# Attention by pairs of heads on two-bank PSUM tiles, Mish on two chunks at once, and a new order of steps

## The chip, the cores and the metric

The kernel runs on one core of a Trainium2 chip. A core has five engines with an instruction queue each: TensorE (PE; PEld is its weight load), VectorE (DVE), ScalarE (ACT), GpSimd (POOL) and SyncE (SP), which here issues the DMAs. The metric is the time of one execution on the device in microseconds (us), as the median of several runs.

## What is computed

Eight batches of eight heads, 576 tokens, 64 features a head. Heads 0 to 3 look back over the last 32 tokens, heads 4 to 7 over every fourth of the last 128. The result, 4608 tokens by 512 features, goes through a feed-forward network with the Mish activation.

```python
scores = scale * np.matmul(q, k.transpose(0, 1, 3, 2))
rel = pos[:, None] - pos[None, :]
mask_plain = (rel >= 0) & (rel < window)                        # 32, heads 0-3
mask_dil = (rel >= 0) & (rel < window * dilation) & (rel % dilation == 0)   # 4, heads 4-7
scores = np.where(masks[None, :, :, :], scores, -1000000000.0)
attn = softmax(scores)                                          # + 1e-9 in the denominator
x = (attn @ v).transpose(0, 2, 1, 3).reshape(B * S, H * D)      # 4608 x 512
h = x @ w_in                                                    # 512 -> 2048
g = h * np.tanh(log1p(exp(h)))                                  # Mish
out = g @ w_out                                                 # 2048 -> 512
```

## The kernel before

**Precision.** Inputs and output are fp32. Operands are split into an fp16 high and low part, and a product is three fp16 matmuls (low·high, high·low, high·high), with power-of-two scales (`f`, `s`) from the largest absolute value of each operand.

**Tiling.** The work is cut into 16 units u = 0 to 15, each half a batch (288 tokens, all heads). A unit goes through these steps, each a Python generator that issues its instructions up to the next `yield` when it is called:

- `ld`, `lv`: DMA loads of q, k, v (on SP's queue). `pr`: largest values (`amax`, DVE), their maximum over partitions, the scales, and the fp16 parts of q, k and v. From unit 6 on the maximum over partitions (tile mru) is POOL's `partition_all_reduce`.
- `sp` and `sc`: the matmuls of the scores of a pair of heads (tiles psc), then mask and maximum on DVE. `ex`: exp on ACT. `tp`: fp16 parts of the weights and a DMA transpose. `va`: the product with v (tile pav), the denominator (den on ACT), and its reciprocal and the normalised output (rec, xs on DVE). `tx`: fp16 parts of xs and a DMA transpose into x, the unit's FFN input. `sp` and `tx` go by pairs of heads; `sc`, `ex`, `tp` and `va` by single heads 0 to 7.
- `ff u.fc`: FF1 of one chunk of 128 of the 2048 features: 12 matmuls of 128x128x288, and Mish on ACT into hm. `gt u.j`: the gated value of four chunks in two fp16 parts (ACT and DVE). `fs`: per-unit scales of FF1 and FF2 (fs, sg, fo).
- `fo u.e.j`: FF2, 12 matmuls for output chunk e (of 4) and feature group j (of 4). After j = 3 the sum is evicted into y (ACT, a few on DVE), and `out_T<-y` stores it. y has two buffers.

In units 0 to 3 ("direct") the attention is in fp32 and is transposed on TensorE. Beside these units, 16 parts of the weights are loaded and split (`wl`, `wm`, `ww`, `ws`, `wp`); `ws` gives the scales f_1 and f_o. `kw n` issues n matmuls of zeros that compute nothing and keep TensorE busy.

**Order.** Nothing is reordered by a scheduler: under `tc.manual_schedule` the list ORDER, some 2,700 words written out in the file, is gone through word by word, and each word runs its step to the next yield. Each engine works through its own queue in that order and waits by semaphores.

**PSUM.** Eight banks of 512 fp32 columns: four one-bank tiles in rotation for the attention (tag "a"), and four one-bank tiles f0 to f3 in rotation for FF1 and FF2.

```python
    fbs, f_turn = [ps.tile([P, 512], F32, name=f"f{i}", bufs=1) for i in range(4)], [-1]
```

In the lists of instructions further on, tiles are named by what the program calls them (b0_70 is tile b0), a DMA or instruction by its line.

Of the kernel before, what the change touches and what calls it, by code (L numbers as in the profile page):

```python
# [42 lines left out]
ws0.0 va0.7 va0.7 tx0.0 ws0.0 tp0.4 tx0.0 tp0.5 tp0.4 kw4 tx0.0 ww0.0.0 kw1 tx0.3 tx0.0 tp0.5 kw7 sp0.1 tx0.3 wm0.2.0
kw1 tx0.3 ld1 sc0.2 va0.4 sc0.3 va0.4 kw6 ex0.2 tx0.3 pr1 ex0.3 ex0.2 va0.5 wp0.0.1 tp0.2 va0.4 tp0.2 fs0.0 ex0.3
wp0.0.1 kw16 kw16 kw2 va0.2 wm0.1.0 tp0.3 ww0.2.0 wl0.2.1 va0.2 va0.5 tp0.3 va0.5 va0.2 kw16 kw16 va0.3 ww0.1.0 tx0.2
va0.3 tx0.2 va0.3 fs0.3 kw16 kw1 tx0.1 tx0.2 ww0.1.0 tx0.1 tx0.2 kw11 tx0.1 kw1 sp1.0 tx0.1 wp0.0.0 ff0.12 sc1.0 sc1.1
ex1.0 sp1.1 wp0.0.0 pr1 tp1.0 ff0.13 sc1.3 tp1.0 wl0.1.1 ex1.1 ld2 wm0.2.1 pr1 sc1.2 kw2 pr1 ff0.0 lv2 ex1.3 ww0.2.1
ex1.2 pr1 ff0.12 ff0.15 ww0.2.0 tp1.1 va1.0 tp1.1 ws0.2 ff0.13 va1.0 ff0.15 sp1.3 va1.0 ff0.0 ws0.2 wm0.1.1 ff0.14
sc1.7 wp0.2.0 sc1.6 sp1.2 ff0.14 ww0.2.1 ex1.7 kw2 va1.1 ff0.3 ff0.1 sc1.4 wp0.2.1 ff0.2 sc1.5 ex1.6 va1.1 gt0.3
ww0.1.1 tp1.2 va1.1 kw5 ws0.1 wp0.2.0 ex1.4 ex1.5 tx1.0 tp1.4 tp1.2 wp0.2.1 wl1.3.0 ff0.3 kw6 va1.2 ws0.1 kw9 ff0.8  # L50
tx1.0 ww0.1.1 tp1.4 tx1.0 ff0.2 tp1.5 ff0.9 tx1.0 wp0.1.0 gt0.3 va1.4 ff0.1 kw2 tp1.3 tp1.5 kw1 ff0.11 va1.2 wp0.1.0
va1.4 wp0.1.1 va1.2 wl1.3.1 tp1.3 wp0.1.1 wm1.3.0 kw16 va1.3 wl1.1.0 va1.5 fs0.2 va1.5 kw3 ff0.4 wl1.1.1 va1.3 va1.4
gt0.0 va1.3 va1.5 tp1.6 ff0.8 tp1.7 fs0.1 tx1.1 ff0.9 ff0.7 pr2 tp1.6 tp1.7 tx1.1 va1.6 ff0.11 va1.7 ff0.4 tx1.2
ww1.3.0 lv3 ff0.10 va1.6 va1.7 va1.6 wm1.3.1 fs1 ff0.6 tx1.1 ff0.7 va1.7 tx1.2 ww1.3.1 tx1.3 ff0.10 tx1.2 gt0.0 ff0.5
tx1.3 tx1.2 ww1.3.0 tx1.3 sp2.0 tx1.3 gt0.2 pr2 ff1.8 sc2.0 ff0.5 ws1.3 sc2.1 ff1.8 ff0.6 gt0.2 gt0.1 ff1.10 pr2
wm1.1.0 ws1.3 pr2 ff1.0 ex2.0 pr2 ff1.9 gt0.1 ex2.1 ff1.1 ww1.3.1 ff1.0 tp2.0 tp2.1 sp2.1 ff1.10 pr3 ff1.9 ff1.4
wm1.1.1 ld3 tp2.0 sc2.2 ff1.7 wp1.3.0 ww1.1.0 sc2.3 ff1.11 ff1.1 wp1.3.0 ff1.4 ff1.2 tp2.1 ff1.7 ww1.1.0 wl1.2.0
ff1.11 sp2.3 wp1.3.1 ff1.3 ff1.2 ww1.1.1 ex2.2 wp1.3.1 ff1.5 sc2.6 fo0.3.0 wl1.2.1 ww1.1.1 gt1.2 fo0.3.1 ex2.6 ws1.1
sc2.7 ex2.3 wm1.2.0 va2.0 ws1.1 sp3.2 va2.0 fo0.3.2 sc3.4 fs2 tp2.2 wm1.2.1 ww1.2.0 fo0.3.3 va2.0 ex3.4 ww1.2.1 va2.1
gt1.2 ff1.6 ff1.3 sc3.5 ws1.2 ff1.5 ww1.2.0 fo0.3.3 gt1.0 fo0.3.3 ff1.12 va2.1 wp1.1.0 ff1.14 ws1.2 ff1.12 ff1.13  # L60
va2.1 tp2.2 wp1.1.0 va2.2 sp3.1 va2.2 gt1.0 ff1.6 wl1.0.1 wp1.1.1 tp2.3 ff1.15 sc3.2 wp1.2.0 wp1.1.1 fo0.1.0 gt1.1
va2.2 wl1.0.0 fo0.1.1 sc3.3 tp2.3 gt1.1 ff1.15 tp2.6 va2.3 tp2.6 sp3.0 va2.3 ff1.14 va2.3 tx2.0 sc3.1 fo1.3.0 tx2.0
ff1.13 sc3.0 ex3.3 va2.6 fo1.3.1 tx2.0 wp1.2.0 va2.6 ex2.7 sp2.2 ww1.2.1 wm1.0.0 tp2.7 fo0.1.2 wm1.0.1 fo0.1.3 tp2.7
ww1.0.1 gt1.3 ww1.0.0 fo1.1.0 fo0.1.3 sc2.5 fo0.1.3 fo1.3.2 sc2.4 ld4 va2.6 ex2.4 fo0.2.0 gt1.3 ex2.5 ww1.0.1 ws1.0
# [154 lines left out]
def attn_mish_ffn_kernel(  # L219
# [692 lines left out]
    def ff2(u, e, j):  # L912

        d = U[u]
        if j == 0:
            d["po", e] = f_next()
# [88 lines left out]
```

## Time and profile before

| what | value |
|---|---|
| median of 3 runs | 925.51 us (925.34 to 926.61) |
| span of the profiled execution | 923.6 us, 22682 instructions; its own time is not listed |
| granted TensorE clock | 0.999 |
| busy: PE, PEld | 913.6 us (99%), 738.9 us |
| busy: DVE, ACT, POOL | 648.8 us (70%), 563.4 us (61%), 17.5 us (2%) |
| FF1 matmuls (L869), FF2 matmuls (L920) | 394.8 us, 390.0 us, 3072 of each |
| keep-warm matmuls (L948) | 492 |
| Mish (L874), gate on ACT (L908) | 256 x 0.496 us, 64 x 1.253 us |

The span reaches from the first to the last instruction of the core; the time of a run also holds what lies around it. A row of a group reads: line, engine, operation, output<-input, shapes, count | busy us, mean ns | idle time of the engine before them, and what ended it. Timeline rows begin with the start and the length in us.

### The profile page before, as it was taken

The page shows a single profiled execution, that of the slowest core. Times are in us where ns is not written, and L with a number is a line of the kernel's source. Part 1 is how long each engine was busy: PE and PEld are TensorE (multiplying, and loading weights), DVE is VectorE, ACT ScalarE, POOL GpSimd, SP SyncE. Part 2 cuts the span into 40 slices and gives each one's busy share as a digit, 9 for nine tenths or more (in the row PEclk, how much of TensorE's full clock was granted, in tenths as well). Part 3 has the DMA queues.
Part 4 walks back from the last instruction along what each step waited for, and adds up shares of the span by engine and source line. Part 5 has one row for each costly group of instructions (what it writes and reads, how often), then busy time and mean ns, then how long its engine had stood idle before and what let it go on. Part 6 is the DMA issues. An engine that isn't in the chain of part 4 may idle for free.

```text
span 923.6 us, 22682 instructions
## 1 busy us (share of the span) xinstructions
PE 913.6 (99%) x9432; PEld 738.9 (80%) x9432; DVE 648.8 (70%) x1353; ACT 563.4 (61%) x1071; POOL 17.5 (2%) x97
## 2 busy tenths in 40 slices
PE   9999999999999999999999999999999999999997
PEld 8878878887778787878787887878788888888875
DVE  4899989758784886898887888777778574623120
ACT  3788967556774566586665665748555664554331
POOL 1000000200000000000000000000000000000000
PEclk9999999999999999999999999999999999999999
DMA  8757322230424325164415242543436033232100
GB/s 252 215 157 245 125 99 66 72 89 2 121 36 123 83 64 117 29 148 82 123 44 118 77 118 51 99 91 99 91 71 120 22 55 55 41 67 35 40 2 26
DMA packets 158103, 82.42 MB, mean 89 GB/s; under 512 B 124496, under 2 KB 153904, under 8 KB 158000
## 3 DMA queue, kind: packets, MB, share of 16 engines
q1 hardware_dynamic: 158000, 80.97, 36.0%
q8 instruction: 74, 1.21, 0.5%
q14 instruction: 29, 0.24, 0.1%
HBM read 49.02 MB, written 9.44 MB: 63 GB/s over the span
## 4 chain that ended last, share of the span: by engine, by line
PE 96%; DVE 1%; DMA 1%; ACT 1%; issue 0%; SPq 0%; ACTq 0%; DVEq 0%
PE f L920 40%; PE f L869 40%; PE psc L628 4%; PE pav L770 3%; PE f L948 3%; PE pav L764 1%; PE ptp L743 1%; DMA qn<-in_qT 1%; PE psc L677 1%; PE psc L625 0%; DMA g<-p 0%; PE pm L374 0%; PE pm L371 0%; ACT y L932 0%; DVE raw L405 0%; DVE raw L403 0%
## 5 line engine op out<-in xcount | busy, mean ns | idle before, releaser
L869 PE MATMUL f<-x,w 128*128 128x288 f16 x3072 | 394.8, 286 | 0.0
L920 PE MATMUL f<-g,w 128*128 128x288 f16 x3072 | 390.0, 286 | 0.0
L920 PEld LDWEIGHTS <-w 128*128 128x128 f16 x3072 | 296.4, 98 | 74.1
L869 PEld LDWEIGHTS <-w 128*128 128x128 f16 x3072 | 294.3, 98 | 73.6
L874 ACT ACTIVATE hm<-f,fs 128x288 f32<-128x288 f32 x256 | 120.7, 496 | 105.7 <-PE f L869 104.3
L910 DVE SCALAR_TENSOR_TENSOR g<-hm,sg,g 128x1152 f16<-128x1152 f32 x64 | 90.0, 1412 | 52.1 <-ACT g L908 52.1
L932 ACT ACTIVATE y<-f,fo 128x288 f32<-128x288 f32 x60 | 42.2, 719 | 93.6 <-PE f L920 74.5
L908 ACT ACTIVATE g<-hm,sg 128x1152 f16<-128x1152 f32 x64 | 80.1, 1253 | 0.9
L785 DVE RECIPROCAL rec<-den 96x3 f32<-96x3 f32 (+1 forms) x128 | 21.5, 168 | 74.9 <-ACT den L781 64.5
L662 DVE TENSOR_TENSOR sb<-sb,nm 96x256 f32<-96x256 f32 (+4 forms) x120 | 54.5, 454 | 4.1
L787 DVE TENSOR_TENSOR xs<-pav,rec 96x192 f32<-96x192 f32 (+1 forms) x128 | 49.6, 387 | 10.4
L660 DVE TENSOR_REDUCE nm<-sb 96x2 f32<-96x256 f32 (+4 forms) x120 | 53.7, 448 | 3.3
L696 ACT ACTIVATE sb<-sb,ln_p 96x352 f32<-96x352 f32 (+3 forms) x96 | 53.0, 584 | 0.2
L781 ACT ACTIVATE den<-pav 96x3 f32<-96x3 f32 (+1 forms) x96 | 14.8, 163 | 60.4 <-PE pav L770 60.4
L654 DVE SCALAR_TENSOR_TENSOR sb<-psc,sc,m_r 96x352 f32<-96x352 f32 (+1 forms) x48 | 28.4, 591 | 24.9 <-PE psc L628 24.9
L802 ACT CAST g<-xs 96x384 f16<-96x384 f32 (+1 forms) x48 | 26.7, 563 | 21.4 <-DVE xs L787 19.3
L543 ACT ACTIVATE q<-qn,s 128x144 f16<-128x144 f32 (+1 forms) x60 | 30.6, 588 | 10.9 <-DVE s L309 10.9
L948 PE MATMUL f<-zeros 128*128 128x128 f16 x492 | 35.1, 229 | 1.0 <-DVE zeros L944 1.0
L654 DVE SCALAR_TENSOR_TENSOR sb<-psc,sc,m_s 72x288 f32<-72x288 f32 (+1 forms) x48 | 27.6, 574 | 11.9 <-PE psc L628 11.9
L628 PEld LDWEIGHTS <-q 64*72 64x72 f16 (+1 forms) x1008 | 26.4, 115 | 10.0 <-issue 8.3
L804 DVE TENSOR_TENSOR g<-xs,g 96x384 f16<-96x384 f32 (+1 forms) x48 | 29.2, 616 | 7.1 <-ACT g L802 6.8
L734 DVE TENSOR_TENSOR p<-sb,p 96x352 f16<-96x352 f32 (+3 forms) x57 | 29.3, 524 | 6.4 <-ACT p L732 6.4
(136 smaller groups left out, 880.4 us busy)
## 6 DMA issues: line engine op xcount, KB each, us to landing
qn<-in_qT SPq DMA_DIRECT2D x16, 576.0 KB
out_T<-y SPq DMA_DIRECT2D x64, 144.0 KB
raw<-in_w_in SPq DMA_DIRECT2D x16, 512.0 KB
raw<-in_w_out SPq DMA_DIRECT2D x16, 512.0 KB
vn<-in_v SPq DMA_DIRECT2D x48, 128.0 KB
vdn<-in_vd SPq DMA_DIRECT2D x32, 104.0 KB
knd<-in_kdT SPq DMA_DIRECT2D x16, 208.0 KB
knp<-in_kT SPq DMA_DIRECT2D x8, 320.0 KB
```

The source lines that it names most:

```text
L628: nc.tensor.matmul(o, q, k, start=start, stop=stop, skip_group_check=True)
L654: nc.vector.scalar_tensor_tensor(shaped(sb), shaped(pt), d["sc"][:nq], mask, ALU.mult, ALU.add)
L660: nc.vector.tensor_reduce(nm[:nq, j:j + n], x, axis=AX.X, op=ALU.max, negate=True)
L662: nc.vector.tensor_tensor(o, x, nm[:nq, j:j + n].unsqueeze(2).broadcast_to([nq, n, w]), op=ALU.add)
L696: nc.scalar.activation(x, x, AF.Exp, bias=ln_p[:nq])
L787: nc.vector.tensor_tensor(xs[:nq, :nb, (head % 2) * D:(head % 2 + 1) * D], avv[:, :, :D], rc.unsqueeze(2).broadcast_to([nq, nb, D]), op=AL ...
L869: nc.tensor.matmul(ph[:, :HT], w1[j][:, c, wi, k * P:(k + 1) * P], x_of(d, xi, c), start=(n == 0), stop=(n == len(seq) - 1))
L874: nc.scalar.activation(d["m"][j][:, k], ph[:, :HT], AF.Mish, scale=d["fs"][:, j:j + 1])
L908: nc.scalar.activation(g[:, 0], m, AF.Identity, scale=sg)
L910: nc.vector.scalar_tensor_tensor(g[:, 1], m, sg, g[:, 0], ALU.mult, ALU.subtract)
L920: nc.tensor.matmul(po[:, :HT], w2[:, e, j, wi, k * P:(k + 1) * P], d["g"][j][:, gi, k, :], start=(j == 0 and n == 0), stop=(j == NCH - 1 a ...
L948: nc.tensor.matmul(fbs[3][:, 512 - P:], zeros, zeros, start=True, stop=True)
```

## The change

- **PSUM**: the eight banks become four tiles b0 to b3 of two banks (`[P, 2, 512]`), shared by everything on TensorE. Which tile a step takes is written in the list (`sp0.2=0` takes b0).
- **Attention by pairs**: `sc`, `ex`, `tp`, `va` work on a pair of heads, one in each half of a tile, with one instruction on ACT or DVE where there were two, and a DMA transpose of twice the size (48 for 96).
- **FF1 by two chunks**: a step holds 2 x 12 matmuls, one chunk in each half, and one Mish on 128x576. **FF2**: outputs e = 0 and 1 (2 and 3) share a tile, one half each; y is evicted half by half, as before 128x288.
- **fs, sg, fo** go from DVE to POOL from unit 0 (fs, sg) and unit 3 (fo) on; sg comes from a precomputed g_1.
- q is scaled in fp32 first (ACT, 128x1152) and then cast, 3 casts in place of 5 operations. Masks are kept in full width. Tables that were empty or uniform (WAYS, ON_POOL) are gone.
- **ORDER** is new, 2049 words for 2675, with 301 keep-warm matmuls for 492: 245 for 446 ahead of the first FF1. Instructions in all: DVE 877 for 1355, ACT 751 for 1071, POOL 161 for 103, SP 374 for 422; the other matmuls are the same.

```diff
+    banks = [ps.tile([P, 2, 512], F32, name=f"b{i}", bufs=1) for i in range(4)]
+    turns, place = {}, []
+    def take(name, tiles):
+        turns[name] = place[0] if place else (turns.get(name, -1) + 1) % len(tiles)
+        return tiles[turns[name]]
...
-        nc.vector.tensor_scalar(d["fs"][:, c], f_1[:, c], d["f_v"], None, ALU.mult)
-        nc.vector.reciprocal(d["sg"][:, c], d["fs"][:, c])
-        nc.vector.tensor_scalar(d["sg"][:, c], d["sg"][:, c], G_SHIFT, None, ALU.mult)
+        nc.gpsimd.tensor_scalar(d["fs"][:, c], f_1[:, c], d["f_v"], None, ALU.mult)
+        nc.gpsimd.tensor_scalar(d["sg"][:, c], g_1[:, c], d["s_v"], None, ALU.mult)
         if u >= FIRST:
-            nc.vector.tensor_scalar(d["fo"], f_o, d["f_v"], 1.0 / G_SHIFT, ALU.mult, ALU.mult)
-    def ff1(u, fc):
+            nc.gpsimd.tensor_scalar(d["fo"], f_o, d["f_v"], 1.0 / G_SHIFT, ALU.mult, ALU.mult)
+    def ff1(u, fp):
+        j, k0 = divmod(2 * fp, FPC)
+        ph = take("b", banks)
...
+        for h in range(2):
+            k = k0 + h
+            for n, (wi, xi, c) in enumerate(seq):
+                nc.tensor.matmul(ph[:, h, :HT], w1[j][:, c, wi, k * P:(k + 1) * P], x_of(d, xi, c),
+                                 start=(n == 0), stop=(n == len(seq) - 1))
+            yield
+        nc.scalar.activation(d["m"][j][:, k0:k0 + 2], ph[:, :, :HT], AF.Mish, scale=d["fs"][:, j:j + 1])
...
     def ff2(u, e, j):
-        if j == 0:
-            d["po", e] = f_next()
-        po = d["po", e]
+        if (e, j) == (e & 2, 0):
+            d["po", e // 2] = take("b", banks)
+        po = d["po", e // 2][:, e % 2]
...
     def keep_warm(n):
+        warm = take("b", banks)
         for _ in range(n):
-            nc.tensor.matmul(fbs[3][:, 512 - P:], zeros, zeros, start=True, stop=True)
+            nc.tensor.matmul(warm[:, 1, 512 - P:], zeros, zeros, start=True, stop=True)
...
-fo15.1.2 fo15.0.3 fo15.1.3 fo15.2.0 fo15.2.1 fo15.2.2 fo15.2.3 fo15.3.0 fo15.3.1 fo15.3.2 fo15.3.3 fo15.3.3 fo15.1.3
+fo15.2.3 fo15.3.0 fo15.3.1 fo15.3.2 fo15.1.3 fo15.1.3 fo15.2.3 fo15.2.3 fo15.3.3 fo15.3.3 fo15.0.3 fo15.3.3
```

Three places of the order are shown, as the engines' queues hold it.

The end of the program on TensorE, where step fo15.3.3 follows fo15.3.2 (weight loads left out); before:

```order
L920 MATMUL f3_111<-g0_112,w2_103 128x288
...
L920 MATMUL f3_111<-g1_113,w2_103 128x288
```

and now, where e = 2 and e = 3 are the halves of b2:

```order
L868 MATMUL b2_72<-g2_114,w2_106 128x288
...
L868 MATMUL b2_72<-g1_113,w2_106 128x288 [waits Activation_49]
```

The same place on ACT, the evictions y of unit 15; before:

```order
L932 ACTIVATE y_13580<-f3_111,fo_12146 128x4x72 [waits DMAHW6_49,PE_49]
L932 ACTIVATE y_13582<-f1_109,fo_12146 128x4x72 [waits DMAHW7_49]
L932 ACTIVATE y_13586<-f2_110,fo_12146 128x4x72 [waits DMAHW0_49,Activation_49]
L932 ACTIVATE y_13589<-f0_108,fo_12146 128x4x72 [waits DMAHW1_49,Activation_49]
```

and now:

```order
L882 ACTIVATE y_11923<-b1_71,fo_10651 128x4x72 [waits DMAHW6_49,PE_49]
L882 ACTIVATE y_11997<-b1_71,fo_10651 128x4x72 [waits DMAHW7_49]
L882 ACTIVATE y_12000<-b2_72,fo_10651 128x4x72 [waits DMAHW0_49,PE_49,Activation_49]
L882 ACTIVATE y_12015<-b2_72,fo_10651 128x4x72 [waits DMAHW1_49,PE_49,Activation_49]
```

The y that stood in one block behind the last matmul now come two before fo15.2.1 to fo15.3.3 and two around fo15.3.3: y_12000 (e = 2) waits for the last matmul of fo15.3.2, and the first matmul of fo15.3.3, on the other half of b2, waits for y_12000. At ten earlier places an FF2 matmul waits in the same way for a y that waits for the matmul just before it.

POOL around unit 13 and 14 (the first ISA of a pair loads a library, the row with mru is the reduction); before:

```order
L563 MEMSET vdh 104x16
L525 ISA mru<-m 128x5
L510 MEMSET m 128x5
L562 MEMSET vh 128x12
```

and now:

```order
L821 ISA
L821 TENSOR_SCALAR fs<-f_107,f 128x4
L822 TENSOR_SCALAR sg<-g_108,s 128x4
L824 TENSOR_SCALAR fo<-f_o,f 128x4
L487 ISA
L487 ISA mru<-m 128x6
L472 MEMSET m 128x6
```

The scales of unit 13 and two rows without operands (ISA) have come in ahead of the reduction of unit 14, and fo waits for an eviction y of unit 9 whose scale tile it takes over.

TensorE at the start; before, behind 234 keep-warm matmuls:

```order
L948 MATMUL f3_111<-zeros_122 128x128
L371 LDWEIGHTS ones_106
L371 MATMUL pm_398<-w13_102,ones_106 128x512 [waits DVE_49]
```

and now, behind 45:

```order
L897 MATMUL b0_70<-zeros_122 128x128
L590 LDWEIGHTS ident_b_96 [waits Activation_49]
L590 MATMUL b0_70<-m_fb_94,ident_b_96 72x288 [waits Activation_49]
...
L593 MATMUL b0_70<-knd_141,qn_137 72x72 x7
L346 LDWEIGHTS ones_110
L346 MATMUL b1_71<-w13_105,ones_110 128x512 [waits DVE_49]
```

The maximum over the weights (L371, now L346) stands behind the first scores, and these (L590) wait for the mask m_fb that ACT writes.

More of the change, by code (lines that the diff above doesn't have):

```diff
@@ L43 @@
[L43 to L52, printed above, removed]
@@ L319, in over_partitions @@
     def over_partitions(m, n):
-        pm = ps.tile([P, 512], F32, tag="a", name="pm", bufs=4)
+        pm = take("b", banks)[:, 0]
         nc.tensor.transpose(pm[:n, :P], m, ident)
@@ L364, in w_scale @@
         n = 1 if k == 0 else NCH
-        pm = ps.tile([P, 512], F32, tag="a", name="pm", bufs=4)
+        pm = take("b", banks)[:, 0]
         for i in range(NCC):
@@ L590, in blocks, with biased @@
         return out
-    def biased(u, head):
-        return (u, head) in BIASED and u not in PE_SUBTRACTS
+    def biased(u, pair):
+        return (u, pair) in BIASED and u not in PE_SUBTRACTS
     def scores_of_pair(u, pair):
@@ L601, in scores_of_pair @@
         width = sum(x[2] for x in bl)
-        pts, heads = [], []
+        pt2 = d["ps", pair] = take("b", banks)
+        heads = []
         for h in range(2):
-            pt = d["ps", 2 * pair + h] = ps.tile([P, 512], F32, tag="a", name="psc", bufs=4)
-            pts.append(pt)
+            pt = pt2[:, h]
             hs, col, products = slice(h * D, (h + 1) * D), 0, []
@@ L693, in exps @@
+        if biased(u, pair):
+            for h in range(2):
+                c = 0
+                for j, (_, _, nk, _, _) in enumerate(bl):
+                    nc.scalar.activation(x[:, h, c:c + nk], pt[:nq, h, c:c + nk], AF.Exp, scale=1.0 / math.sqrt(D),
+                                         bias=nm[:nq, h, j:j + 1])
+                    c += nk
         elif d["direct"]:
@@ L735, in transpose_p @@
             yield
-            pT = in_rotation(1, pTs)
-            nc.sync.dma_start_transpose(pT[:, :2 * nb * rows].rearrange("k (g q) -> k g q", q=rows), p16[:rows, :2 * nb * P])
-            d["p", head] = pT
+            pT = take("pT", pTs)
+            nc.sync.dma_start_transpose(pT[:, :4 * nb * rows].rearrange("k (g q) -> k g q", q=rows), p16[:rows, :4 * nb * P])
+            d["p", pair] = pT
             return
-        pt = ps.tile([P, 512], F32, tag="a", name="ptp", bufs=4)
-        col = 0
-        for _, q0, nk, _, _ in bl:
-            nc.tensor.transpose(pt[:nk, q0:q0 + nq], sb[:nq, col:col + nk], ident[:nq, :nq])
-            col += nk
-        pp = d["p", head] = pool.tile([P, HT], F32, name="pp", bufs=2)
+        pt = take("b", banks)
+        for h in range(2):
+            col = 0
+            for _, q0, nk, _, _ in bl:
+                nc.tensor.transpose(pt[:nk, h, q0:q0 + nq], sb[:nq, h, col:col + nk], ident[:nq, :nq])
+                col += nk
+        pp = d["p", pair] = early.tile([P, 2, HT], F32, name="pp", bufs=2)
         yield
-        if head < 4 and d["half"] == 0:
+        if pair < 2 and d["half"] == 0:
             runs = [(QB, 0, QB), (P, QB, HT)]
@@ L809, in transpose_x @@
             return
-        px = ps.tile([P, 512], F32, tag="a", name="px", bufs=4)
+        px = take("b", banks)[:, 0]
         for i, (_, q0, _, _, j) in enumerate(bl):
```

573 lines of the change are left out of this document (259 added, 314 removed), and 7 rows, old and new, of tables (ON_ACT, WAYS).

## The prediction, made before the changed kernel was run

> **What bounds the kernel now.** I read the page first: busy times, then the chain that ended last.
>
> ```profile
> PE 913.6 (99%) x9432; PEld 738.9 (80%) x9432; DVE 648.8 (70%) x1353; ACT 563.4 (61%) x1071; POOL 17.5 (2%) x97
> PE 96%; DVE 1%; DMA 1%; ACT 1%; issue 0%; SPq 0%; ACTq 0%; DVEq 0%
> L948 PE MATMUL f<-zeros 128*128 128x128 f16 x492 | 35.1, 229 | 1.0 <-DVE zeros L944 1.0
> ```
>
> TensorE is the bound, from end to end; the keep-warm matmuls (L948) are the part of its time that computes nothing. Next the stretches (columns: us and instructions of PE, PEld, DVE, ACT, POOL; clock, DMA share, GB/s) and TensorE's waits.
>
> ```profile
> 0.00:16.70 16.70, 15.65 (x235) 15.66 (x236) 6.12 (x9) 4.37 (x6) 2.85 (x17) 1.00 0.81 244
> 16.70:49.50 32.80, 32.63 (x430) 27.79 (x428) 27.43 (x66) 22.95 (x48) 0.25 (x2) 1.00 0.72 226
> 49.50:111.00 61.50, 61.50 (x605) 49.78 (x605) 58.39 (x122) 53.71 (x100) 0.48 (x3) 1.00 0.56 169
> 160.00:869.70 709.70, 709.39 (x7324) 569.52 (x7322) 506.99 (x1062) 432.58 (x822) 13.91 (x75) 1.00 0.35 77
> ```
>
> ```profile
> PE pav L764 <- ACT pp L752: 1.6, 1, 1.6
> PE f L948 <- DVE zeros L944: 1.0, 1, 1.0
> PE pav L770 <- DMA g<-p: 0.3, 1, 0.3
> PE psc L677 <- DVE nm L660: 0.2, 1, 0.2
> ```
>
> TensorE waits 3.1 us in all, and in the 710 us of the long middle stretch it is idle 0.3 us. No FF1 or FF2 matmul waits for an eviction anywhere. So every wait that the change puts in front of a matmul counts in full, and only keep-warm, idle time and the tail can be saved. DVE (649) and ACT (563) have room; making them shorter gains nothing by itself.
>
> ```profile
> 1.05 15.75 PE f L948 x234
> 40.76 1.90 PE f L948 x34
> 893.19 23.53 PE f L920 x192
> 917.54 1.74 DMA out_T<-y
> 919.93 0.77 ACT y L932
> ```
>
> These are pieces of the chain (start, us, what). A later keep-warm matmul is 1.90/34 = 0.056 us; twelve FF matmuls are 23.53/16 = 1.47 us. Keep-warm in all: 15.75 + 258 × 0.056 = 30.2 us. The median of the runs is 925.5; the profiled execution has span 923.6, and its own time isn't listed, so 1.9 us are taken as lying around the span, and the sum goes from 925.5.
>
> **Term 1, the two-bank tiles in FF2: a new wait.** Eviction y of output e reads one half of a tile while the other half's matmuls go on. The built program orders by whole tiles: the list of instructions with waits has places where the next FF2 matmul waits for y although it writes the other half, and y itself waits for the matmul just before. There are eleven such places (ten y on ACT, one on DVE); the last is shown above, before fo15.3.3. Nothing can cover such a place: TensorE's queue is in order, and all that is behind it waits too.
>
> ```profile
> 869.76 0.78 ACT L932 ACTIVATE y<-f,fo 128x288 f32<-128x288 f32 x1 [2.53 <-PE f L920]
> L932 ACT ACTIVATE y<-f,fo 128x288 f32<-128x288 f32 x60 | 42.2, 719 | 93.6 <-PE f L920 74.5
> L934 DVE TENSOR_SCALAR y<-f,fo x4: 516/518/518, 145.6 to 186.5; 128x288 f32<-128x288 f32 x4
> ```
>
> One y is 0.78 us from an idle ACT, and I estimate 0.07 for the two hand-offs: 0.85; on DVE 0.52 + 0.07 = 0.6. The nine on ACT ahead of the tail and the one on DVE: 9 × 0.85 + 0.6 = 8.2 us, so +8.2. Lower end: 0, if ordering by tile costs nothing there; upper end: ACT is busy 433 of 710 us, and where a gate (1.25, below) is just ahead, a place is 2.1: 9 × 2.1 + 0.6 = 19.5. I stay near the bare price, since the four instructions ahead of y on ACT at these places wait for things that end well before.
>
> The Trainium skill ("PSUM — Partial Sum Buffer", section PSUM bank collisions raise a hardware error) wants two engines kept apart by bank and quadrant. The two halves are two banks, so by that rule no wait is needed here, and the sum would be 8.2 us lower, 923.8. No run here shows a program without these waits; the semaphores are in the one that runs, and they decide.
>
> **Term 2, the tail.** Before:
>
> ```profile
> 916.75 1.29 ACT L932 ACTIVATE y<-f,fo 128x288 f32<-128x288 f32 x2 [21.73 <-PE f L920]
> 919.37 1.33 ACT L932 ACTIVATE y<-f,fo 128x288 f32<-128x288 f32 x2 [1.32 <-DMA out_T<-y]
> ```
>
> All four y of unit 15 come after the last matmul (916.73), and the last two wait for a y buffer until an out_T has landed; the end is 923.6. So from the end of fo15.3.2 (1.47 earlier, 915.26) to the end: 8.3. After: y of e = 0 and 1 are out earlier; after fo15.3.2 comes y of e = 2 (0.80), then fo15.3.3 (1.47), beside which its out_T lands (1.78 with the hand-off; e = 3 takes the same buffer), then y of e = 3 (0.78), then the last out_T (923.6 − 920.7 = 2.9): 6.3. That is −2.1, with the eleventh bubble in it. Ends: −2.6 and −1.0.
>
> **Term 3, the start and the early stage.** The list has 301 keep-warm matmuls for 492: 245 for 446 ahead of the first FF1, 56 for 46 behind it.
>
> ```profile
> 0.87 0.39 POOL L271 MEMSET m_f<- 96x352 f32 x1
> 11.94 0.28 POOL masks.py:199 TENSOR_SCALAR_AFFINE_SELECT ident<-ident 128x128 f32<-128x128 f32 x1 [10.68 <-issue]
> 13.72 0.48 ACT L282 ACTIVATE m_fb<-m_f 96x352 bf16<-96x352 f32 x1
> 16.63 1.06 PE L371 MATMUL pm<-w,ones 128*128 128x512 bf16 x4
> ```
>
> The first real matmul started at 16.63, held by 234 keep-warm ones; now the 45 of the start are gone after some 5 us, and TensorE waits for m_fb, ready at 14.2: 2.4 us earlier. Behind that stand 256 against 258 keep-warm matmuls, so the 191 that are taken out are worth 2.4 us here, not 191 × 0.056 = 10.7: the rest becomes idle time. If 2.1 us of the old waits go too, the early stage gains 4.5. Against it: all scales of unit 0 (fs0, on POOL) now wait for the fourth group's f_1, so the first Mish does too. Ahead of it DVE has eight word shifts, six pairs of raw, four splits and the pair-wide reductions:
>
> ```profile
> 8.76 0.69 DVE L401 TENSOR_SCALAR w<-w 128x1024 int32<-128x1024 int32 x1 [7.77 <-ACT w L360]
> L405 DVE SCALAR_TENSOR_TENSOR raw<-raw 128x1024 int32<-128x1024 int32 x6 | 7.4, 1226 | 0.2
> L422 DVE SCALAR_TENSOR_TENSOR w<-raw,ws,w 128x1024 f16<-128x1024 f32 x4 | 5.1, 1272 | 0.0
> ```
>
> 8 × 0.7 + 12 × 1.23 + 4 × 1.27 + some 21 for the small ones = 46 us from 8.8 on, and 2 to 3 of waits: first Mish at 57 or 58. TensorE, with three pairs of chunks and the attention of unit 0 before it, arrives about then; up to 3 us would be lost. Ends −4.5 and +3; I take −2. TensorE also sits idle about 9 us at the start. The Trainium skill ("TensorE: Matmul & The Clock Gate", HAM oscillation) warns of idle gaps over about 3.4 µs, after which the clock is halved for a time; by it a microsecond or so more would be lost, and the trace of before has no such gap to show it (its first 234 matmuls took 67 ns each, the later ones 56).
>
> **Term 4, scales on POOL.** fs, sg and fo move from DVE to POOL, where partition_all_reduce (mru) also runs. The two belong to different libraries: the instruction list has a load (ISA) before each change, 13 in place of 2. Only one is not covered by my reading: at fo13/mru14. fo13 waits for y of fo9.3.3; then load, mru14, m, f, s on DVE, and qn, q, k on ACT behind s; den, rec and xs of va12.1 are queued behind these; sp13.2 on TensorE needs that tile.
>
> ```profile
> 655.76 0.38 POOL L525 PARTITION_ALL_REDUCE mru<-m  x1 [12.02 <-DVE m L313]
> L908 ACT ACTIVATE g<-hm,sg 128x1152 f16<-128x1152 f32 x64 | 80.1, 1253 | 0.9
> L543 ACT ACTIVATE q<-qn,s 128x144 f16<-128x144 f32 (+1 forms) x60 | 30.6, 588 | 10.9 <-DVE s L309 10.9
> L549 ACT ACTIVATE k<-knd,s 128x576 f16<-128x576 f32 (+1 forms) x12 | 10.4, 871 | 0.0
> L309 DVE RECIPROCAL s<-f 128x3 f32<-128x3 f32 (+1 forms) x16 | 2.8, 173 | 0.5
> L787 DVE TENSOR_TENSOR xs<-pav,rec 96x192 f32<-96x192 f32 (+1 forms) x128 | 49.6, 387 | 10.4
> ```
>
> y 0.78, fo about 0.2, mru 0.38, four small ones 0.7, the 128x1152 scaling 1.25, three casts 1.8, two k 1.7, den and rec 0.3, xs twice 0.39: 7.9 us and the load R. TensorE has between fo9.3.3 and sp13.2 six times 1.47 and 0.5 of pav: 9.4. So R − 1.5 is lost. R is bounded by 0 and by the 10.68 of the start, where DMA was busy all the time: 0 to 9.2. From the middle, R = 5, I take +3.5. The Trainium skill ("GPSIMD Engine Reference", 2.1 Instruction dispatch) gives ≈6 µs for a load; by it this term would be 4.5 and the sum 933.1. No row of before shows a load outside the start.
>
> **Costed at nothing**: Mish on 128x576 (half the instructions, about 0.75 us by the rows' 0.50 for 128x288) under the next pair's matmuls, 2.9 us; q scaled first and then cast; the pair-wide exps and casts, since ACT and DVE have room; the transposes of p, 48 of twice the size, whose one wait in the trace was 0.3 us (SP has 374 rows to issue for 422, so its queue gets no longer).
>
> Sum: 925.5 + 8.2 − 2.1 − 2 + 3.5 = 933.1; with the early stage's better half as likely as not, I say 932.
>
> **Rivals.**
> 1. Faster: the early stage gives back what the bubbles take. All 191 keep-warm matmuls would have to count: 925.5 + 8.2 − 2.1 − 10.7 = 920.9. It decides from an early gain of 8 us. For it: DVE and ACT issue fewer instructions there. Against: TensorE was full from 49.5 on, and m_fb holds its start. 0.14.
> 2. Much the same: reload hidden (R under 1.5), early gain 4.5: 925.5 + 8.2 − 2.1 − 4.5 = 927.1. For it: DMA, which the load needs, is busy 0.35 there, not 0.81. 0.15.
> 3. Much slower: the reload in full, no early gain, and ACT busy so often that a place costs 1.3 on average: 925.5 + 12.3 − 2.1 + 9.2 = 945; with one of these milder, 936 to 945. 0.18.
> 4. The waits on the other half cost nothing, since both halves are done when TensorE comes: 923.8, as worked out under term 1. Against it: at each of the eleven places y waits for the matmul just before. 0.05.
> 5. The forecast, 927.4 to 936, most likely 932: 0.48.
>
> Under 0.2% (1.9 us) a change can't be told from none. Faster holds rival 1, same rivals 2 and 4, slower the rest: 0.14, 0.20, 0.66. The range, 922 to 941, leaves out the outer parts of rivals 1 and 3.
>
> **What would show it.** In the profile after: waits of TensorE at L868 for ACT y L882, ten of about 0.85 us, and one for DVE y; these absent, or 0.2 long, and term 1 is wrong. y of e = 0 and 1 of unit 15 ahead of the last FF2, end 5 us after the last matmul. First real matmul at about 14.2 after an idle stretch, first Mish near 58. A gap in POOL ahead of mru14 and a wait of sp13.2 (L593) of R − 1.5. The forecast falls if TensorE shows waits elsewhere, at L741 for transposes or at L837 for Mish.

## The result, and the profile after

The changed kernel takes 966.79 us (median of three runs, 965.08 to 968.32), the kernel before 925.42 beside it (four runs, 925.34 to 926.61). A fourth run of the changed kernel took 1910.91 us, for a reason that is not known, and is left out; with it the median would be 967.56, the 967.6 from which the expectations below reckon. The ratio is 1.0444 (95% interval 1.0427 to 1.0460): slower, as forecast, but by 41 us where some 7 were forecast, and above the range. The profiled run took 965.08 us; its span is 963.3, against 923.6.

The page of the profile first: busy times, the chain, and the group of the FF2 matmuls.

```profile
PE 911.9 (95%) x9238; PEld 730.6 (76%) x9241; DVE 591.0 (61%) x875; ACT 524.3 (54%) x751; POOL 47.2 (5%) x144
PE 84%; DVE 6%; ACT 3%; DMA 3%; issue 2%; SPq 2%; POOL 0%; ACTq 0%; DVEq 0%; POOLq 0%
L868 PE MATMUL b<-g,w 128*128 128x288 f16 x3072 | 394.8, 289 | 30.3 <-ACT y L882 25.7
```

TensorE is as busy as before (911.9 us for 913.6) in a span 39.7 us longer, and on the chain that ended last it fell from 96 to 84%. DVE and ACT did become lighter (591 for 649, 524 for 563); the time rose all the same. The 30.3 us of idle time in front of FF2 are new. TensorE's waits, the largest five (total, times, longest):

```profile
PE b L868 <- ACT y L882: 25.7, 12, 7.1
PE b L590 <- ACT m_fb L249: 5.2, 1, 5.2
PE b L593 <- DVE xs L756: 4.5, 1, 4.5
PE b L868 <- ACT den L751: 2.0, 2, 1.2
PE b L868 <- DVE y L880: 1.8, 2, 1.2
```

All waits together are 47 us, against 3.1. Twelve waits for y on ACT make 25.7, and they are far from equal: one is 7.1. The two waits for den belong to y as well: at both places den (525.53 and 752.04) stands right behind a y on ACT, and both waits are gone in e9 below, where these y are moved. The gaps in TensorE's queue, with their sizes in brackets:

```profile
298.78 6.08 PE L868 MATMUL b<-g,w 128*128 128x288 f16 x36 [5.84 <-ACT y L882]
356.47 7.71 PE L868 MATMUL b<-g,w 128*128 128x288 f16 x48 [3.95 <-ACT y L882]
582.35 7.43 PE L868 MATMUL b<-g,w 128*128 128x288 f16 x48 [7.06 <-ACT y L882]
699.82 1.25 PE L593 MATMUL b<-k,q 64*72 64x104 f16 x24 [4.51 <-DVE xs L756]
957.75 1.63 PE L868 MATMUL b<-g,w 128*128 128x288 f16 x12 [0.90 <-ACT y L882]
```

Three long waits for y (of units 3, 4 and 8, outputs 1, 2 and 2) make 16.85; the others on ACT are 0.24 to 1.75 each. What y itself waited for is told by ACT's rows. At the first and the third place, ACT (and DVE at the first):

```profile
293.21 1.07 DVE L617 SCALAR_TENSOR_TENSOR sb<-b,sc,m_d 72x832 f32<-72x832 f32 x1
294.32 1.02 DVE L623 TENSOR_REDUCE nm<-sb 72x8 f32<-72x832 f32 x1
295.37 1.02 DVE L625 TENSOR_TENSOR sb<-sb,nm 72x832 f32<-72x832 f32 x1
...
296.43 0.99 ACT L664 ACTIVATE sb<-sb,ln_p 72x832 f32<-72x832 f32 x1 [1.14 <-DVE sb L625]
297.45 0.89 ACT L700 CAST g<-sb 72x832 f16<-72x832 f32 x1
298.24 0.49 ACT L882 ACTIVATE y<-b,fo 128x288 f32<-128x288 f32 x1
...
577.04 1.87 ACT L664 ACTIVATE sb<-sb,ln_p 72x832 f32<-72x832 f32 x2 [4.64 <-DVE sb L625]
578.94 0.89 ACT L700 CAST p<-sb 72x832 f16<-72x832 f32 x1
579.73 0.77 ACT L664 ACTIVATE sb<-sb,ln_p 72x576 f32<-72x576 f32 x1
580.53 0.67 ACT L700 CAST p<-sb 72x576 f16<-72x576 f32 x1
581.11 0.51 ACT L772 CAST x<-xs 96x384 f16<-96x384 f32 x1
581.52 0.77 ACT L882 ACTIVATE y<-b,fo 128x288 f32<-128x288 f32 x1
```

The matmul before y ended at 292.9, but y ran at 298.24: ahead of it in ACT's queue stood the exp of scores that TensorE had only just issued, and the exp waited for DVE (three operations of 1 us each, L617, L623, L625). At 577 it is the same with three exps. At the second place y waited for something else; the chain there (start, us, what):

```profile
349.07 0.81 DVE p L702
349.89 0.42 SPq L777
...
350.41 1.26 SPq L705
...
351.77 3.80 DMA out_T<-y
...
355.65 0.78 ACT y L882
```

Here y needs a free y buffer. The store out_T of an earlier y stood in SP's queue behind two DMA transposes (L777, L705) that waited for DVE. So a wait on DVE reached TensorE by way of SP, a DMA and ACT.

The stretches around these places (us; busy PE, PEld, DVE, ACT, POOL; then the granted clock, DMA share, GB/s):

```profile
200.00:280.00 80.00, 80.00 (x787) 63.74 (x784) 54.52 (x82) 47.95 (x59) 2.32 (x3) 1.00 0.26 66
280.00:320.00 40.00, 34.16 (x373) 26.87 (x369) 22.95 (x30) 17.77 (x27) 0.80 (x7) 0.91 0.46 113
340.00:360.00 20.00, 16.05 (x170) 12.18 (x168) 14.32 (x18) 8.87 (x13) 3.54 (x8) 0.91 0.43 64
560.00:600.00 40.00, 32.94 (x289) 25.63 (x288) 19.03 (x23) 19.69 (x26) 2.86 (x11) 0.91 0.38 73
680.00:720.00 40.00, 35.49 (x347) 28.00 (x345) 22.16 (x31) 14.47 (x23) 0.89 (x4) 0.91 0.34 91
```

With no gap TensorE is full at clock 1.00; in each stretch with one of the four long gaps the clock falls to 0.91. The 48 FF2 matmuls behind the gap of 7.06 took 7.43 us and those behind 3.95 took 7.71; where no gap is ahead (below) 48 take 6.04. The 36 behind 5.84 took 6.08, where e6b below has 4.57. So a long gap costs some 1.5 us more than itself.

The difference of the spans: waits +44; keep-warm 18.8 us (4.53 for the first 45, 0.056 for each of the other 256) for 30.2, so −11.4; the tail −3.0 behind the last matmul. That makes 29.6, and 10.1 us are left to 39.7. The matmuls behind the three long waits for y account for 4.6 of them; the gap of 4.51 and the start (clock 0.83 from 0 to 20 us) add to it, by how much is not resolved.

Then the rows that the prediction named for terms 2, 3 and 4, in order of time:

```profile
1.56 0.29 POOL masks.py:199 TENSOR_SCALAR_AFFINE_SELECT ident<-ident 128x128 f32<-128x128 f32 x1 [0.30 <-POOL m_f L238]
...
57.87 0.30 POOL L821 TENSOR_SCALAR fs<-f,f 128x4 f32<-128x4 f32 x1 [54.12 <-DVE f L357]
...
62.81 0.74 ACT L840 ACTIVATE hm<-b,fs 128x576 f32<-128x576 f32 x1
...
693.03 0.41 POOL L487 PARTITION_ALL_REDUCE mru<-m  x1 [5.90 <-issue]
...
946.59 1.31 ACT L882 ACTIVATE y<-b,fo 128x288 f32<-128x288 f32 x2 [9.73 <-PE b L868]
...
959.64 0.77 ACT L882 ACTIVATE y<-b,fo 128x288 f32<-128x288 f32 x1 [1.94 <-DMA out_T<-y]
```

### The profile page after: what moved, and what is told of

The parts are those of the page before. It is cut to its first block, busy times and chain, and to the rows that moved or that the text cites. A ratio compares the mean times of both kernels' runs of the same rounds, so it can differ in the third digit from the quotient of the medians.

```text
span 963.3 us, 21451 instructions
## 1 busy us (share of the span) xinstructions
PE 911.9 (95%) x9238; PEld 730.6 (76%) x9241; DVE 591.0 (61%) x875; ACT 524.3 (54%) x751; POOL 47.2 (5%) x144
## 4 chain that ended last, share of the span: by engine, by line
PE 84%; DVE 6%; ACT 3%; DMA 3%; issue 2%; SPq 2%; POOL 0%; ACTq 0%; DVEq 0%; POOLq 0%
PE b L837 36%; PE b L868 35%; PE b L593 4%; PE b L741 3%; PE b L897 1%; PE b L735 1%; DMA knd<-in_kdT 1%; ACT y L882 1%; DVE xs L756 1%; DVE g L858 1%; PE b L712 1%; DMA vn<-in_v 1%; DMA out_T<-y 1%; DMA vdn<-in_vd 1%; PE b L590 1%
## 5 line engine op out<-in xcount | busy, mean ns | idle before, releaser
L868 PE MATMUL b<-g,w 128*128 128x288 f16 x3072 | 394.8, 289 | 30.3 <-ACT y L882 25.7
L837 PE MATMUL b<-x,w 128*128 128x288 f16 x3072 | 386.8, 287 | 0.0
L840 ACT ACTIVATE hm<-b,fs 128x576 f32<-128x576 f32 x128 | 92.7, 736 | 103.9 <-PE b L837 94.5
L882 ACT ACTIVATE y<-b,fo 128x288 f32<-128x288 f32 x60 | 42.0, 717 | 139.6 <-PE b L868 116.2
L664 ACT ACTIVATE sb<-sb,ln_p 96x704 f32<-96x704 f32 (+3 forms) x48 | 42.2, 890 | 45.2 <-DVE sb L625 45.1
L625 DVE TENSOR_TENSOR sb<-sb,nm 96x512 f32<-96x512 f32 (+4 forms) x60 | 45.2, 754 | 2.1
L623 DVE TENSOR_REDUCE nm<-sb 96x4 f32<-96x512 f32 (+4 forms) x60 | 44.9, 748 | 1.7
L756 DVE TENSOR_TENSOR xs<-b,rec 72x512 f32<-72x512 f32 (+1 forms) x64 | 39.7, 620 | 6.0
L702 DVE TENSOR_TENSOR p<-sb,p 96x704 f16<-96x704 f32 (+3 forms) x31 | 27.7, 898 | 18.6 <-ACT p L700 18.5
L617 DVE SCALAR_TENSOR_TENSOR sb<-b,sc,m_r 96x704 f32<-96x704 f32 (+1 forms) x24 | 23.4, 976 | 21.3 <-PE b L593 21.0
L593 PE MATMUL b<-k,q 64*96 64x128 f16 (+3 forms) x1008 | 31.6, 212 | 4.5 <-DVE xs L756 4.5
L617 DVE SCALAR_TENSOR_TENSOR sb<-b,sc,m_d 72x576 f32<-72x576 f32 (+1 forms) x24 | 22.6, 943 | 10.8 <-PE b L593 10.4
```

The costliest lines, as they stand in the source:

```text
L593: nc.tensor.matmul(o, q, k, start=start, stop=stop, skip_group_check=True)
L617: nc.vector.scalar_tensor_tensor(args[0], args[1], d["sc"][:nq], args[2], ALU.mult, ALU.add)
L623: nc.vector.tensor_reduce(nm[:nq, :, j:j + n], x, axis=AX.X, op=ALU.max, negate=True)
L625: nc.vector.tensor_tensor(blocked(sb, c0, n, w), x, nm[:nq, :, j:j + n].unsqueeze(3).broadcast_to([nq, 2, n, w]), op=ALU.add)
L756: nc.vector.tensor_tensor(xs[:nq, :nb].rearrange("p j (h e) -> p h j e", h=2), avv[:, :, :, :D], rc.unsqueeze(3).broadcast_to([nq, 2, nb, ...
L837: nc.tensor.matmul(ph[:, h, :HT], w1[j][:, c, wi, k * P:(k + 1) * P], x_of(d, xi, c), start=(n == 0), stop=(n == len(seq) - 1))
```

## The experiments

Two readings were weighed. One: the time goes into y standing in order behind things that are not ready, with a slow clock behind long gaps; move y, and the time comes back. The other: the four shared two-bank tiles are too few, so that the wait comes back at whichever step takes the tile next. Each edit is told against the changed kernel (where nothing else is said), and "before" ran beside each on the same chip (925.38 to 925.52); the changed kernel did not, so its 966.79 is from its own measurement. In words of the list, `fo u.e.3` issues in turn the matmuls, y and the store.

**e1_y_later and e1b_three: y behind the sister's matmuls.** In e1 every y that stood ahead of the last matmuls of the other half of its tile is moved behind them, in e1b three of them (the first shown):

```diff
-fo3.1.2 fo3.1.3 fo3.1.3 fo3.2.3 fo3.0.1 fo3.0.2 fo3.0.3 fo3.0.3
+fo3.1.2 fo3.1.3 fo3.2.3 fo3.0.1 fo3.0.2 fo3.0.3 fo3.1.3 fo3.0.3
```

> In the list, each eviction y that stood ahead of FF2 matmuls of the other half of its tile (31 of 64) now stands behind the last of them; nothing else changes. Theory A (TensorE waits because y of one half orders the matmuls of the other, and y is stuck in ACT's queue): the waits of L868 for y (25.7 us on ACT, 1.8 on DVE) and the two for den (2.0) go, and with the three long ones the slow clock behind them (about 1.7 us each): 967.6 - 29.5 - 5 = 933. Rival B (the coarser steps and the new order stall TensorE anyway): the waits come back at the next user of the tile or at L593 and L741, and the time stays above 950.

Measured: 953.41 us (952.40 to 955.01), ratio 1.0304 (1.0289 to 1.0319): not the theory's 933. No FF2 matmul waited for y any more, but new waits had come, which speaks for the rival as far as this run goes. A likely reason is that some of the moved y had held nobody and, moved, release their tiles and results later; e5 and e9 below bear on it. Of the four largest behind the start, the first was there before (4.5, at sp13.2), the other three are new:

```profile
PE b L592 <- DVE xs L755: 5.1, 1, 5.1
PE b L592 <- ACT den L750: 3.7, 1, 3.7
PE b L740 <- DMA pT<-p: 3.2, 1, 3.2
PE b L348 <- DVE w L376: 3.0, 1, 3.0
```

> Only the three y with the long waits (unit 3 e=1, unit 4 e=2, unit 8 e=2; 5.84, 3.95 and 7.06 us) are moved behind the other half's last matmul. Theory A: 16.9 us of waits and about 5 us of slow clock go: 967.6 - 22 = 946; the short ones (0.85 to 1.75 each) stay. Rival B (these three are late for a reason that holds TensorE a step later as well): 960 or more.

Measured: 944.74 us (943.33 to 946.53), ratio 1.0210 (1.0194 to 1.0225): 22.1 us from three moved y, 16.85 of them the waits themselves. In 280 to 320, 340 to 360 and 560 to 600 us TensorE is now full at clock 1.00, so most of the other 5 is the clock (4.6 by the rows above; the expectation was 946). At these three places no wait came back.

**e6a_out_first and e6b_exp_behind: the three causes by themselves.** y stays where it is. In e6a the store ahead of the second place goes in front of the two transposes in SP's queue; in e6b exp and casts at the first and third place go behind y.

```diff
 # e6a
-tx5.2=1 tx5.2 tx5.2 ex6.0 tp6.0=1 tp6.0 tp6.0=2 sc7.2 fo4.0.3 fo4.0.3 fo4.0.3
+tx5.2=1 tx5.2 ex6.0 tp6.0=1 tp6.0 sc7.2 fo4.0.3 fo4.0.3 fo4.0.3 tx5.2 tp6.0=2
 # e6b (first place)
-ex5.2 tp5.2=0 tx4.3 fo3.1.2 fo3.1.3 fo3.1.3
+tx4.3 fo3.1.2 fo3.1.3 fo3.1.3 ex5.2 tp5.2=0
```

> Against the changed kernel only the third words of tx5.2 and tp6.0 (two DMA transposes on SP) are put behind the out_T of unit 4, e=0. Theory E (y of unit 4, e=2 waited 5.44 us for a y buffer, because that out_T stood in SP's queue behind transposes that waited for DVE): its FF2 wait falls from 3.95 to about 0.9, the slow clock behind it (1.8) goes: 967.6 - 4.9 = 962.7. Rival (the wait is the tile's, not the buffer's): 3.95 stays, 967.6.

> Against the changed kernel only ex5.2 and tp5.2 are put behind y of unit 3, e=1, and ex11.2, ex11.3, ex10.2 with their casts behind y of unit 8, e=2, so that in ACT's queue y isn't behind an exp that waits for DVE. The order by tiles stays. Theory F (these two waits of 5.84 and 7.06 us are ACT's queue, and the order by tiles alone costs 0.85 a place): they fall to 0.9 each, with 1.7 of slow clock each: 967.6 - 11.1 - 3.4 = 953. Rival (the wait is due to the tile order itself, however y is queued): no change.

Measured: e6a 963.80 us (962.36 to 965.21), ratio 1.0413 (1.0399 to 1.0426), 3.0 less than the change, which the intervals barely separate; e6b 952.93 (952.39 to 955.09), ratio 1.0293 (1.0278 to 1.0308), 13.9 less. Both are within 1.1 us of what was expected. The places, first in e6a, then in e6b:

```profile
356.44 6.04 PE L867 MATMUL b<-g,w 128*128 128x288 f16 x48 [0.33 <-ACT y L881]
```

```profile
294.46 4.57 PE L867 MATMUL b<-g,w 128*128 128x288 f16 x36 [1.48 <-ACT y L881]
...
572.33 6.04 PE L867 MATMUL b<-g,w 128*128 128x288 f16 x48 [0.86 <-ACT y L881]
```

3.95 became 0.33, 5.84 became 1.48, and 7.06 became 0.86, which is the bare price of the prediction. That a queue ahead of y made the long waits is thereby shown, for each by its own cause.

**e4_kw_in_gaps: the clock.** 60, 40 and 80 keep-warm matmuls are put in front of the three waits. They compute nothing and only shorten the idle stretch.

```diff
-fo3.1.3 fo3.2.3 fo3.0.1
+fo3.1.3 fo3.2.3 kw60=0 fo3.0.1
```

> 60, 40 and 80 keep-warm matmuls are put in front of the FF2 matmuls that wait 5.84, 3.95 and 7.06 us (a tile that is free is taken); no wait is shortened, but TensorE idles only some 2.5 us at each. Theory D (a gap over about 3.4 us sets the clock to half for a while): the 14, 48 and 48 matmuls behind the gaps, which now take 1.6 to 1.8 us too long each, run at full speed: 967.6 - 5 = 962.5. If the slow matmuls behind a gap have another reason: 967.6, no change.

Measured: 965.61 us (962.03 to 968.22), ratio 1.0437 (1.0404 to 1.0469); 5 us less were expected, and by the time alone this can't be told from the change. The matmuls behind the first and the third wait:

```profile
299.46 6.24 PE L867 MATMUL b<-g,w 128*128 128x288 f16 x36 [2.49 <-ACT y L881]
580.67 6.04 PE L867 MATMUL b<-g,w 128*128 128x288 f16 x48 [2.59 <-ACT y L881]
```

At the third, idle for 2.59 us in place of 7.06, the same 48 matmuls took 6.04 us, not 7.43. At the second the keep-warm matmuls filled the wait, and 48 took 6.04, not 7.71. So the slow matmuls there came of TensorE's idle time. But at the first, 36 still took 6.24 us behind a gap of 2.49 (full speed is 4.57); that is 1.7 us of the gain that is missing. The length of the gap alone doesn't settle it: in the thirteen traces of this case the clock fell behind every gap of 2.98 us or more, stayed at 1.00 behind single gaps of up to 1.5, and went either way between 1.58 and 2.59 (behind 1.85 us in e6a 36 matmuls took 6.24, behind 1.93 in e4 they took 4.57). The Trainium skill ("TensorE: Matmul & The Clock Gate", HAM oscillation) has the rule that no idle gap be over about 3.4 µs. The slow matmuls behind 1.85 and 2.49 us don't agree with that as a safe limit, and the measurement decides.

**e2_scales_dve: fs, sg, fo back on DVE.**

```diff
-        nc.gpsimd.tensor_scalar(d["fs"][:, c], f_1[:, c], d["f_v"], None, ALU.mult)
+        nc.vector.tensor_scalar(d["fs"][:, c], f_1[:, c], d["f_v"], None, ALU.mult)
```

(and the same for sg and fo).

> fs, sg and fo of every unit are computed on DVE instead of POOL. Theory C (library loads on POOL cost 5.9 us at fo13/mru14): the wait of sp13.2 for xs (4.5 us) and the slow clock behind it (1.7) go. The first load at the start, which is not seen in the trace after (affine_select at 1.56 us, before at 11.94), comes back if it hangs on which library the run before left in POOL; then m_fb is ready at 14.2 instead of 10.7: +3.5. Sum 967.6 - 6.2 + 3.5 = 965. If the start doesn't hang on that: 961. If loads don't matter: 967.6.

Measured: 964.13 us (963.68 to 967.05), ratio 1.0425 (1.0409 to 1.0441): 2.7 less than the change, which the intervals don't separate (965 was expected). The wait of sp13.2 fell from 4.5 to 0.6, but the load at the start came back, and TensorE waits 8.8 us for m_fb in place of 5.2:

```profile
11.77 0.28 POOL masks.py:199 TENSOR_SCALAR_AFFINE_SELECT ident<-ident 128x128 f32<-128x128 f32 x1 [10.50 <-issue]
```

**e5_moved_waits, e7_start_kw, e9_two_back: all waits for y.** e5 moves only the 16 y for which TensorE did wait (14, and the two ahead of den), as e1 does, and puts fs13 behind mru14. e7 is e5 with 64 keep-warm matmuls more at the start. e9 is e5, but (0,1) and (1,2) stay where they were.

```diff
 # e5, and the moves of y as above
-fo9.3.3 fo9.3.3 fo9.3.3 fs13 pr14 ff11.2=0 tp12.0=1 ff11.2 pr14 ff11.2
+fo9.3.3 fo9.3.3 fo9.3.3 pr14 ff11.2=0 tp12.0=1 ff11.2 pr14 fs13 ff11.2
 # e9 against e5
-fo1.2.3 fo1.3.0 fo1.3.1 fo1.3.2 fo1.3.3 fo1.2.3
+fo1.2.3 fo1.2.3 fo1.3.0 fo1.3.1 fo1.3.2 fo1.3.3
```

> The 16 evictions y for which TensorE was seen to wait (unit and e: 0.1, 1.2, 3.1, 4.2, 5.1, 6.3, 7.1, 7.2, 8.2, 11.1, 11.2, 12.1, 12.2, 13.2, 14.2, 15.2) stand behind the other half's last matmul; the other 15 stay where they were. And fs13 (POOL) is put behind the reduction mru14, so that no library load stands ahead of mru14. Theories A and C: from the kernel with three y moved (944.7) another 12.8 us of short waits and 4.6 + 1.7 of the load go: 925.6, level with the kernel before. Rival B (a y moved back makes a new wait a step later, as in the kernel with all 31 moved): above 933.

> The kernel with 16 y moved and fs13 behind mru14, and 64 more keep-warm matmuls at the start, so that TensorE isn't idle between 5.6 and 10.7 us. Theory D: the granted clock of the first 20 us (0.83) goes to nearly 1, and the first steps are 1 to 2 us shorter: 924. Rival (DMA and DVE bound the first 50 us, a slow TensorE there costs nothing): no difference to the kernel without them, 925.6.

> As e5, but y of (0,1) and (1,2) stay where the changed kernel has them. Theory: moving these two made TensorE wait 3.1 us for the word shifts of a weight part on DVE at 154.8 (with 1.4 us of slow clock behind it), which cost more than their waits of 0.6 and 1.2: 933.2 + 1.8 - 4.5 = 930.5. Rival: that wait comes from another place in the early stage and stays, and the two waits are added: 935.

Measured: e5 933.21 us (931.25 to 936.86), ratio 1.0088 (1.0072 to 1.0103); e7 934.54 (933.63 to 936.59), 1.0100 (1.0087 to 1.0113); e9 928.23 (926.42 to 931.11), 1.0032 (1.0022 to 1.0041). e5 missed its 925.6 and fell on the rival's side: a new wait in the early stage, for the word shifts of a weight part on DVE, with a slow clock behind it. e7 gained nothing in time, but a gap of 2.22 us was left in front of m_fb, and the clock of 0 to 20 us rose only from 0.70 in e5 to 0.83; what a full clock would be worth there stays open. In e9 the new wait of e5 is gone, and it gained 5.0, more than the 2.7 expected. The wait of sp13.2 is 0.3 in e5 and e9: that the load ahead of mru14 made it is shown. The row of e5, and then TensorE's waits and the long stretches of e9:

```profile
154.75 1.86 PE L348 MATMUL b<-w,ones 128*128 128x128 bf16 x16 [3.10 <-DVE w L376]
```

```profile
PE b L589 <- ACT m_fb L248: 5.1, 1, 5.1
PE b L867 <- DVE y L879: 1.8, 2, 1.2
...
200.00:500.00 300.00, 299.69 (x3162) 240.50 (x3161) 217.88 (x309) 181.84 (x243) 16.55 (x45) 1.00 0.39 86
500.00:900.00 400.00, 399.62 (x4048) 321.25 (x4046) 223.98 (x305) 209.89 (x286) 10.27 (x50) 1.00 0.31 67
```

Fourteen moved y and one moved fs13 take 38.6 of the 41.4 us back. From 200 to 900 us TensorE is idle 0.7 us, on the same four shared tiles: they are not too few, which is where the second reading falls. e9 is still 0.3% slower than the kernel before, and its waits stand almost all in the first 180 us.

**e8_tail_before and e10_tail_kw: parts of the change on the kernel before.** e8 gives the kernel before the new order of the tail, on its one-bank tiles; e10 takes 32 keep-warm matmuls at the start away as well (`kw16 kw16`).

```diff
-fo15.3.2 fo15.3.3 fo15.3.3 fo15.1.3 fo15.3.3 fo15.1.3 fo15.2.3 fo15.2.3 fo15.0.3 fo15.0.3
+fo15.3.2 fo15.2.3 fo15.2.3 fo15.3.3 fo15.3.3 fo15.3.3
```

(y and stores of outputs 0 and 1 among fo15.2.0 to fo15.2.3).

> The kernel before with one part of the change alone, the order of the tail: y of e = 0 and 1 of unit 15 and their stores come among the last FF2 steps, y of e = 2 ahead of fo15.3.3 and y of e = 3 behind it. On one-bank tiles no matmul waits for a y of another output. Theory (term 2 of the prediction was right, and its gain does not need two-bank tiles): behind the last matmul remain one y (0.8) and one out_T (2.9), 3.7 us where there were 6.9, so 925.4 - 3.1 = 922.3. Rival: the last y still waits for a y buffer until the out_T of e = 1 or 2 has landed, as before (1.3 there), so 923.6 or more.

> As e8, and 32 of the 234 keep-warm matmuls at the start (2.1 us by 67 ns each) taken out. Theory (term 3: the start of the first real matmul counts): the words' maximum (L371) starts near 14.7 in place of 16.6 and all follows: 922.3 - 1.9 = 920.4. Rival (what the 64 keep-warm matmuls of e7 pointed to: DVE's and the DMAs' chains set the early stage, not TensorE's queue): the idle time comes back some us later and the time stays at 922.3.

Measured: e8 922.12 us (921.55 to 922.19) against 925.38 (924.00 to 926.33), ratio 0.9961 (0.9947 to 0.9974); e10 922.39 (919.97 to 922.62), 0.9957 (0.9945 to 0.9970). e8 is the version that beats both kernels, and came out where term 2 puts it. Its tail:

```profile
899.83 16.82 PE L917 MATMUL f<-g,w 128*128 128x288 f16 x136
...
916.74 0.77 ACT L929 ACTIVATE y<-f,fo 128x288 f32<-128x288 f32 x1 [5.10 <-PE f L917]
```

The last matmul ends at 916.65 and the span at 920.4, 3.75 us later, where there were 6.9. Of e10 the time says no gain, as the rival had it. But its first real matmul did start at 14.57 us (15.98 in the profile of e8), and later its profiled run lost time to a slow clock:

```profile
126.82 0.72 PE L761 MATMUL pav<-vn,pp 128*96 128x65 f32 x6 [1.58 <-ACT pp L749]
...
129.42 2.76 PE L866 MATMUL f<-x,w 128*128 128x288 f16 x12
```

In e8 the gap at this place is 1.59 us, and the same 12 matmuls took 1.64. Two of e10's five runs, 919.97 and 920.36, are below all of e8's; these two have a granted clock of 1.000, the other three 0.998. So some 2 us were won where the clock stayed full, about what was expected. That the clock made the difference in the runs without a profile is not shown.

## Why the prediction was right or wrong

**Bound, direction.** Right: TensorE bounds the kernel, and a wait put in front of it counts in full (e1b). That lighter DVE and ACT gain nothing fits every run and was not tried by itself.

**Term 1.** The mechanism was right (in e6b one place costs 0.86), its size was not. The ten places ahead of the tail were put at 8.2 us; the waits for y ahead of the tail are 13 and measure 26.6 (25.7 + 1.8, less the tail's 0.9), over the upper end of 19.5; three places had not been counted. The step that failed is "I stay near the bare price, since the four instructions ahead of y on ACT at these places wait for things that end well before". At units 3 and 8 they were exps of scores issued just before, held by three operations on DVE, and at unit 4 it was the y buffer, held by a store behind transposes on SP: 5.84, 7.06 and 3.95 us in place of 0.85 each, 14.3 too little. The upper end looked only at an ACT that is busy, not at one that waits. The other places came to 0.24 to 1.75.

**The slow clock.** It was put at nothing in the sum; only a sentence on the start named it, with a microsecond or so. Behind waits of about 0.85 us, as I had priced them, the clock stays at 1.00; behind the three long ones it did not, so the error in term 1 brought a second one with it: 1.4 to 1.7 us behind each of the three long waits at the matmuls themselves, and with the start and the gap of 4.51 at most 10.1 by the bookkeeping above.

**Term 2.** Right: from the end of fo15.3.2 (956.85) to the end of the span 6.45 us, where 6.3 was worked out; e8 shows the part without bubble, −3.3 (925.38 to 922.12), for which −3.1 was expected.

**Term 3.** Net −2.1 by waits and keep-warm (31.2 us for 33.3), where −2 was said, but by another way, so the agreement is luck: m_fb was ready at 10.7, not 14.2, for want of a library load at the start, and TensorE still waited 5.2 us for it, then ran at a low clock. The scales of unit 0 came at 57.87, when the first Mish had been expected; it followed only at 62.81, and no matmul waited for it.

**Term 4.** Right: a load of 5.90 us ahead of mru14 and 4.5 us lost at sp13.2, by R − 1.5 from the measured load 4.4; I took 3.5. By the ≈6 µs that the Trainium skill ("GPSIMD Engine Reference", 2.1 Instruction dispatch) gives for a load it was 4.5, and the trace agrees, with 5.90 for this load. The sum by it would be 934.1, not the 933.1 that the prediction gives for it.

**Costed at nothing.** Mish on 128x576 took 0.74 us and held nobody. Not covered were one wait for the gate at FF2 (0.8 us) and the two named by den (2.0 us), which are waits for y, as shown above.

**Rivals.** Rival 3 had the right sign and the right engine (ACT), but its places were 1.3 us on average where the twelve on ACT came to 2.1. Rival 4, by which the two banks keep the halves apart, is refuted by the waits: the program orders by tile, and the wait is in its semaphores. Rivals 1 and 2 needed an early gain of 8 and 4.5 us that no run shows.

## What to carry to other kernels

Where a change puts a wait in front of the engine that bounds the kernel, price it by reading, at each place, what stands ahead of the releasing instruction in its own engine's queue, and what that waits for in turn, through buffers, stores and DMA queues too; its own duration is only the lower end. A few places make the bill: three of 14 were 16.9 of 27.5 us, and each of these three cost another 1.4 to 1.7 in slow clock. A shorter gap, of 1.6 to 2.6 us, can bring the slow clock too. If two halves of a tile are ordered as one, evict the first half behind the sister's last matmul, but only where TensorE really waits, since moving the rest brought new waits (e1 against e5: 953.4 and 933.2, of which the moved fs13 accounts for some 6).

## What was not expected of the hardware

Whether a kernel pays for a library load at its start goes with the kind of POOL instruction that it ends on. The four kernels whose last such instruction is a `partition_all_reduce` (before, e2, e8, e10) show 10.0 to 10.7 us of idle time ahead of the row with ident; the nine that end on a `tensor_scalar` show 0.30. That the library stays from the execution before is a reading that fits all thirteen, and it was not tried by itself. The later load in the row above is 5.9 us; five others, ahead of fs, are 6.8 to 7.6 in the changed kernel's trace.
